# Two attention layers between two linear-attention layers: side work in pieces of three, an output projection in two parts, and the score bound as a bias of the exponential

## The chip, the cores and the metric

The kernel runs on one core of one Trainium2 chip. The core has a matrix engine (PE), a vector engine (DVE), a scalar engine that evaluates functions such as the exponential (ACT), a general engine (POOL) and an engine that in this kernel only starts transfers (SP). Each of them works through its own list of instructions in order; they wait for each other through semaphores. The metric is the device time of one launch in microseconds (us), lower is better.

## The reference

The input x has 2048 rows of 512 numbers. Four layers are applied one after the other, each to the row-normalized x, and each adds its result to x: attention A, linear attention B, attention A again, B again, with the same weights in both rounds.

```
x = x + A(layernorm(x));  x = x + B(layernorm(x))      (twice)

A:  q, k, v = split(x @ wqkv)                  32 heads of 16
    o = softmax(q k^T / 4) v;   result o @ wo
B:  q, k, v = split(x @ wqkv)
    phi(u) = [softmax(u w_phi), softmax(-u w_phi)]   per head
    kv = phi(k)^T v;  z = sum of phi(k)
    o = phi(q) kv / (phi(q) z + 1e-6);   result o @ wo
```

## The kernel before

**The attention.** The 32 heads are worked in four octets of eight, each octet in two groups of four heads (g = 0 to 7). For a group, the 2048 queries are taken in four blocks j of 512, and the 2048 keys in 16 tiles kt of 128. One (g, j, kt) is a step; a layer has 512 of them. The loop in `attention` (L862) issues for each step `scores` (L807), which is four matmuls of 64 rows into two PSUM tiles, each followed by one exponential on ACT over 128 x 1024 numbers (L816), and then `pvs` (L819) of the step two before (LAG), four matmuls of probabilities with values into one PSUM accumulator. After 16 steps the accumulator is divided by its row of sums on DVE (`norm`, L474); a finished octet's block goes to the DRAM buffer oD. The three PSUM tiles of scores are the only buffer between PE and ACT, so PE can be at most three exponentials ahead.

**The bound of the scores.** The kernel does not look for the maximum. It subtracts half of the squared norm of the query and half of the largest squared norm of a key. The queries, keys and these bounds sit in tiles kq of 64 rows for each head: 48 rows of high and low parts, one row `sh` with the bound (written by DMA, `load_shift`, L802) and 15 rows that are constant (DMA from dC, L781). So the subtraction is done by the score matmul itself, and the exponential has a constant scale and a constant bias of zero. The squared norms come from `square`, `norms`, `key_bound` and `add_bound` (L642 to L667). The lowest bound of every octet goes to `okt`; a flag at the end starts a second, general version of the kernel if a bound is too low.

**Side work.** Between the steps, PE also does what the next octets need, in pieces. `octet(o)` (L678) computes values (pieces of 16 matmuls of 128 x 128) and queries and keys (pieces of 4 x 4 matmuls, each 32 columns wide, L553); `prep_ao` and `prep_b` (first attention only) load, fold, scale and split the weights of the later layers; `tail(j)` (L846) does the output projection of block j over all four octets, adds x and computes the next layer's normalized and transposed input. These generators stand in a queue, `fill`; `pump` (L853) runs the first one up to its next `yield`. A credit grows by `rate` per step (0.38, 0.345 or 0.55) and a whole credit pays for one piece; after the 16th step of a block a piece is run in any case. At step 118 of an octet the rest of the next octet is run without pause and its kq tiles are loaded. All side work shares one PSUM bank, M. The weight preparation works on whole weights, for instance one DVE instruction over 128 x 2048 numbers (L91, L117, L120), right behind the loads that it reads.

**Order.** PE's order in the attention is the order of the program. The order on the other engines and on SP comes from a scheduler at build time; SP issues its transfers strictly in that order. Large tiles come from a pool of 11 buffers (`bigp`), and the tile stg, from which kq is loaded, has one buffer.

**The B layers.** After the last step, `feed` of layer B runs 16 tiles of 128 rows; between its first tiles it runs what is left of tail(3), three pieces of 4 x 4 matmuls for each tile. The end of B feeds the first octet of the next attention (`head`, `head_norms`, `feed_end`).

Of the kernel before, what the change touches and what calls it, by code (L numbers as in the profile page):

```python
# [17 lines left out]
P = 128  # L18
S = 2048
D = 512  # L20
# [10 lines left out]
SHROW = 16.0  # L31
# [4 lines left out]
FILLED = 118  # L36
# [7 lines left out]
def mha_hedgehog_stack(ctx, tc, x_in, a_wqkv, a_wo, b_wqkv, b_wphi, b_wo, out, shmin=SHMIN):  # L44
# [66 lines left out]
    def scale_of(vs, name):  # L111
        return scale_from([peak_of(v, None) for v in vs], name)

# [23 lines left out]
    xd = [tc.dram_tile([S, D], F32, name=f"xd{i}") for i in range(3)]  # L137
    oD = tc.dram_tile([NJ, P, 3, 2, 512], F16, name="oD")

    def split_store(w, sc, dram, name):  # L140
        hl = big([P, 2, NC4, 512], F16, name)
        split((hl[:, 0], hl[:, 1]), w, sc)
        nc.sync.dma_start(dram, hl)
        return hl


    dC = tc.dram_tile([16, 2, S], F16, name="dC")
    c16 = np_.tile([16, 2, 512], F16, tag="yt", name="c16", bufs=3)
    nc.gpsimd.memset(c16[:, 0, :], SHROW)
    nc.gpsimd.memset(c16[:, 1, :], 0.0)  # L150
# [10 lines left out]
    def prep_a():  # L161
# [7 lines left out]
        for j in range(NJ):  # L169
            nc.sync.dma_start(dC[:, :, j * 512:(j + 1) * 512], c16)  # L170
# [31 lines left out]
        with tc.manual_schedule(engines=COMPUTE):  # L202
# [42 lines left out]
            for j in range(1, NJ):  # L245
# [20 lines left out]
                a1.head_norms(j - 1)  # L266
# [9 lines left out]

    def prep_ao():
        wo = load_w(a_wo, "awo")
        es, sc = scale_of([flat(wo)], "sAo")
        split_store(wo, sc, dAo, "ahlo")  # L280
        con["oA"] = out_scale(con["esA"], es, "c_oA")
# [7 lines left out]

    perm_in = lambda ap: ap.rearrange("p (c h q f) -> p c q h f", c=4, h=4, q=2)  # L290
    perm_out = lambda ap: ap.rearrange("p (c q h f) -> p c q h f", c=4, h=4, q=2)

    def prep_b():
# [5 lines left out]
        yield  # L299
        folded = []  # L300
        for i in range(2):
            w = load_w(b_wqkv[:, i * 512:(i + 1) * 512], f"bw{i}")
            wf = big([P, NC4, 512], F32, f"bf{i}")
            for c in range(4):
# [10 lines left out]
                for q in range(2):  # L315
                    nc.vector.tensor_copy(
                        wf[:, :, c * P + q * 64:c * P + q * 64 + 64].rearrange("p n (h f) -> p n h f", f=DH),
                        psf.rearrange("p (n h q f) -> p n h q f", n=NC4, h=4, q=2)[:, :, :, q, :])
                yield
            folded.append(wf)  # L320
        es, sc = scale_of([flat(folded[0]), flat(folded[1])], "sB")
# [3 lines left out]
        for i in range(2):  # L325
            split_store(folded[i], sc, dBqk[:, i], f"bhl{i}")
            yield
        wv = load_w(b_wqkv[:, 1024:1536], "bwv")
        esv, scv = scale_of([flat(wv)], "sBv")
        hl = big([P, 2, NC4, 512], F16, "bhlv")  # L330
        for d in range(NC4):
            src, dh, dl = (perm_in(wv[:, d, :]), perm_out(hl[:, 0, d, :]), perm_out(hl[:, 1, d, :]))
            for c in range(4):
                for q in range(2):
                    split((dh[:, c, q], dl[:, c, q]), src[:, c, q], scv)
            yield
        for a in range(2):
            nc.sync.dma_start(dBv[a], hl[:, a])
        yield
        wo = load_w(b_wo, "bwo")  # L340
        eso, sco = scale_of([flat(wo)], "sBo")
        split_store(wo, sco, dBo, "bhlo")
# [170 lines left out]
    def o_block(j, ob, wo, co, x_src, x_dst, box, after=None, wide=True, early=False, piece=4):  # L513


        for t2 in range(2):
            r = (4 * j + 2 * t2) * P
            xt = xp.tile([P, 2, D], F32, tag="xt", name="xt")
            nc.sync.dma_start(xt, x_src[r:r + 2 * P, :].rearrange("(t p) d -> p t d", p=P))
            if wide:  # L520
                ps2 = psS.tile([P, 2, 512], F32, tag="S", name="po2")
            if early and t2 == 0:
                for cs in ((0,), (1,), (2,), (3,)):
                    for u in range(2):
                        for c in cs:
                            for i, (a, b) in enumerate(PASSES):
                                nc.tensor.matmul(ps2[:, u, :], ob[:, c, a, u * P:(u + 1) * P], wo[:, b, c, :],
                                                 start=(c == 0 and i == 0), stop=(c == NC4 - 1 and i == 2))
            for u in range(0 if early and t2 == 0 else 2):
                t = 2 * t2 + u  # L530
                n = 0
                for a, b in PASSES:
                    for c in range(NC4):
                        if n % piece == 0:
# [3 lines left out]
                        mm_cols(ps, ob[:, c, a, t * P:(t + 1) * P], wo[:, b, c, :], n, not wide)  # L538
# [10 lines left out]
    def mm_cols(ps, w, x, n, cols):  # L549

        for i in range(4 if cols else 1):
            r = slice(32 * i, 32 * i + 32) if cols else slice(0, P)
            nc.tensor.matmul(ps[r, :], w[:, r], x, start=(n == 0), stop=(n == 11), skip_group_check=cols)  # L553
# [29 lines left out]
    class LayerA:  # L583
# [23 lines left out]
        def stage(self, o):  # L607
            self.oct[o].update(
                stg=stgp.tile([P, 4, S], F16, tag="stg", name="stg"),
                sh=np_.tile([32, S], F16, tag="sh", name="sh", bufs=1),  # L610
                km=sp.tile([32, 4], F32, name="km"),
            )

        def project(self, o, j, ps, ten, piece=2):
            n = 0
            for a, b in PASSES:
                for c in range(NC4):
                    mm_cols(ps, self.oct[o]["w"][:, a, ten, c, :], self.xnT[j][:, b, c, :], n, piece == 4)
# [4 lines left out]
        def values(self, o, j, ps):  # L623
# [3 lines left out]
            for t in range(4):  # L627
                for a, b in PASSES:
                    for c in range(NC4):
# [3 lines left out]
                        if n % 16 == 0 and n < 48:  # L633
                            yield
# [7 lines left out]
        def square(self, hi):  # L642
            sq = np_.tile([P, 512], BF16, tag="sq", name="sq", bufs=3)
# [6 lines left out]
        def norms(self, o, j, sq, ten):  # L650
            q = self.oct[o]
            psn = psum1("psn")
            nc.tensor.matmul(psn[0:32, :], bones, sq, start=True, stop=True)
            if ten:
                nc.vector.tensor_reduce(q["km"][:, j:j + 1], psn[0:32, :], AX.X, ALU.max)
            else:
                nc.vector.tensor_scalar(q["sh"][:, j * 512:(j + 1) * 512], psn[0:32, :], -0.5 / SHROW, None, op0=ALU.mult)

        def key_bound(self, o):
            q = self.oct[o]  # L660
            q["hk"] = sp.tile([32, 1], F32, name="hk")
            nc.vector.tensor_reduce(q["hk"], q["km"], AX.X, ALU.max)
            nc.vector.tensor_scalar(q["hk"], q["hk"], -0.5 / SHROW, None, op0=ALU.mult)

        def add_bound(self, o, sl):
            q = self.oct[o]
            nc.vector.tensor_scalar(q["sh"][:, sl], q["sh"][:, sl], q["hk"], None, op0=ALU.add)  # L667

        def end_octet(self, o):
            self.key_bound(o)  # L670
            self.add_bound(o, slice(0, S))
            self.lowest(o)

        def lowest(self, o):
            i = self.li * 4 + o
            nc.vector.tensor_reduce(okt[:, i:i + 1], self.oct[o]["sh"], AX.X, ALU.min)

        def octet(self, o):  # L678
# [4 lines left out]
            for j in range(NJ):  # L683
                yield from self.values(o, j, psum1("pv_"))
                yield
            self.stage(o)
            stg = self.oct[o]["stg"]
            for j in range(NJ):
                for ten in (1, 0):
                    ps = psum1("pqk")  # L690
                    yield from self.project(o, j, ps, ten, 4)
# [6 lines left out]
                    sq = self.square(hi)  # L698
                    yield
                    self.norms(o, j, sq, ten)  # L700
                    if j == 2 and ten == 0:
                        self.alloc_pairs(2 * o)
                        self.load_rows(2 * o, slice(0, 1536))
                    if j < 3 or ten:
                        yield
            self.end_octet(o)
            self.ready = o
# [22 lines left out]
        def head_norms(self, j, tens=(1, 0)):  # L730
            for ten in tens:
                self.norms(0, j, self.sqs.pop((j, ten)), ten)
# [4 lines left out]
        def feed(self, lns, work):  # L737

            for j, (a, b, c) in enumerate(work):
# [4 lines left out]
                if j == NJ - 1:  # L744
                    self.head_norms(2)
# [3 lines left out]
                if 0 < j < NJ - 1:  # L749
                    self.head_norms(j - 1)  # L750
# [9 lines left out]
        def feed_end(self, more=True):  # L760
            self.head_norms(3, (1,))
            if more:
                self.head_values(2)
            self.key_bound(0)
            self.add_bound(0, slice(0, 512))
            self.load_shift(0, slice(0, 512))
            self.head_norms(3, (0,))
            self.head_values(3)
            self.add_bound(0, slice(512, S))
            self.load_rows(0, slice(1536, S))  # L770
            self.load_shift(0, slice(512, S))
            self.lowest(0)
            self.alloc_pairs(1)
            self.load_pairs(1)

        def alloc_pairs(self, g):
            tiles = []
            for pr in range(2):
                t = big([P, 2, S], F16, f"kq{g}_{pr}")
                for s in range(2):  # L780
                    nc.sync.dma_start(t[64 * s + 48:64 * s + 64], dC)  # L781
                tiles.append(t)
            self.kq[g] = tiles

        def load_pairs(self, g):
            self.load_rows(g, slice(0, S))
            self.load_shift(g, slice(0, S))
# [14 lines left out]
        def load_shift(self, g, sl):  # L802
            sh = self.oct[g // 2]["sh"]
# [484 lines left out]
```

## Time and profile before

| | us |
|---|---|
| median of 3 runs (2619.69 to 2622.96) | 2621.23 |
| the profiled execution's own time | 2620.91 |
| its span, first to last instruction | 2619.1 |
| PE busy | 2503.1 |
| ACT busy | 2196.1 |
| DVE busy | 997.4 |
| POOL busy | 371.5 |

Busy times are sums over the span; matmuls are pipelined, so PE's busy time holds overlaps and is no measure of how full it is. Times in rows of the timeline count from the start of the span. In a group's row stand the count, the busy time, the mean duration of one in ns, and the idle time before it with what ended it. A duration is longer than the distance between two starts, since consecutive instructions of an engine overlap a little.

### The profile page before, as it was taken

The page shows a single profiled execution, that of the slowest core. Times are in us where ns is not written, and L with a number is a line of the kernel's source. Part 1 is how long each engine was busy: PE and PEld are TensorE (multiplying, and loading weights), DVE is VectorE, ACT ScalarE, POOL GpSimd, SP SyncE. Part 2 cuts the span into 40 slices and gives each one's busy share as a digit, 9 for nine tenths or more (in the row PEclk, how much of TensorE's full clock was granted, in tenths as well). Part 3 has the DMA queues.
Part 4 walks back from the last instruction along what each step waited for, and adds up shares of the span by engine and source line. Part 5 has one row for each costly group of instructions (what it writes and reads, how often), then busy time and mean ns, then how long its engine had stood idle before and what let it go on. Part 6 is the DMA issues. An engine that isn't in the chain of part 4 may idle for free.

```text
span 2619.1 us, 50234 instructions
## 1 busy us (share of the span) xinstructions
PE 2503.1 (96%) x20960; PEld 812.9 (31%) x20960; DVE 997.4 (38%) x1902; ACT 2196.1 (84%) x2436; POOL 371.5 (14%) x502
## 2 busy tenths in 40 slices
PE   6899999999999899999899999999999999999998
PEld 4322222222223122355343222222222212224543
DVE  6211211221223533689872122112211302338897
ACT  5799999999899899654437999999999999994552
POOL 3000000000000000266430000000000000004552
PEclk8999999999999899999999999999999999999999
DMA  4500220130113411100234003201301230110003
GB/s 147 110 29 9 47 40 5 27 50 11 57 27 84 157 45 46 41 25 1 73 96 67 13 11 51 32 5 28 60 5 26 56 74 32 48 44 26 9 17 106
DMA packets 52414, 120.43 MB, mean 46 GB/s; under 512 B 11024, under 2 KB 14224, under 8 KB 49360
## 3 DMA queue, kind: packets, MB, share of 16 engines
q1 hardware_dynamic: 51504, 114.76, 18.3%
q8 instruction: 166, 2.72, 0.4%
q0 software_dynamic: 672, 2.36, 0.2%
q14 instruction: 72, 0.59, 0.1%
HBM read 60.06 MB, written 31.59 MB: 35 GB/s over the span
## 4 chain that ended last, share of the span: by engine, by line
PE 73%; DVE 12%; ACT 8%; issue 4%; POOL 2%; DMA 1%; ACTq 0%; SPq 0%; POOLq 0%; DVEq 0%
PE pv L831 33%; PE s L813 20%; ACT p L816 6%; PE pqk L553 5%; PE po L553 5%; DVE su L1017 2%; PE pk L946 1%; PE pbv L946 1%; PE pq L946 1%; POOL f L1026 1%; PE pst L419 1%; DVE f L1009 1%; PE pn L1086 1%; DVE su L1018 1%; DVE yt L503 1%
## 5 line engine op out<-in xcount | busy, mean ns | idle before, releaser
L816 ACT ACTIVATE p<-s 128x1024 f32<-128x1024 f32 x2048 | 1907.0, 1075 | 63.9 <-PE s L813 58.0
L831 PE MATMUL pv<-p,v 128*32 128x512 f32 x8192 | 1096.3, 607 | 13.8 <-DVE yt L476 13.7
L813 PE MATMUL s<-kq 64*128 64x512 f16 x4096 | 676.8, 384 | 23.2 <-DMA kq<-sh 2.8
L813 PEld LDWEIGHTS <-kq 64*128 64x128 f16 x4096 | 157.7, 93 | 805.6 <-issue 792.0
L831 PEld LDWEIGHTS pv<-p,v 128*32 128x32 f32 x8192 | 162.4, 108 | 370.9 <-issue 331.6
L645 POOL TENSOR_TENSOR sq<-stg 128x512 bf16<-128x512 f16 x48 | 68.9, 1435 | 1313.0 <-DVE stg L696 1306.1
L695 DVE TENSOR_SCALAR tq<-pqk,c_qk 128x512 f32<-128x512 f32 x48 | 35.1, 732 | 451.3 <-PE pqk L553 451.3
L1026 POOL TENSOR_TENSOR f<-f,su 128x1024 f32<-128x1024 f32 x62 | 120.0, 1935 | 575.7 <-DVE su L1020 547.4
L476 DVE STREAM_TRANSPOSE yt<-pv 128x512 f32<-128x512 f32 x64 | 45.8, 716 | 404.9 <-PE pv L831 404.8
L946 PEld LDWEIGHTS <-xnTa 128*128 128x128 f16 x1152 | 109.6, 98 | 139.8 <-DVE f L1010 14.8
L553 PEld LDWEIGHTS <-wA 128*32 128x32 f16 (+1 forms) x2496 | 86.4, 97 | 149.4 <-issue 100.6
L1011 ACT ACTIVATE f<-f,c_pB 128x1024 f32<-128x1024 f32 x64 | 72.5, 1148 | 38.2 <-DVE f L1010 37.9
L553 PE MATMUL pqk<-xnTb,wA 128*32 128x512 f16 (+1 forms) x1248 | 98.4, 381 | 1.1 <-ACT xnTb L429 1.1
L946 PE MATMUL pbv<-wbv,xnTa 128*128 128x512 f16 x384 | 88.2, 379 | 11.0 <-DVE f L1010 11.0
L553 PE MATMUL po<-woA,ob 128*32 128x512 f16 x1536 | 97.5, 379 | 0.0
L553 PE MATMUL pqk<-xnT,wA 128*32 128x512 f16 (+1 forms) x1224 | 92.4, 379 | 2.7 <-DVE xnT L432 2.2
L1032 ACT ACTIVATE fk<-f 128x1024 f16<-128x1024 f32 x30 | 31.7, 1057 | 74.9 <-POOL f L1026 74.9
L541 DVE SCALAR_TENSOR_TENSOR xt<-po,c_oA,xt 128x512 f32<-128x512 f32 x32 | 23.2, 724 | 183.9 <-PE po L553 183.9
L946 PE MATMUL pq<-wbqk,xnTa 128*128 128x512 f16 x384 | 88.4, 379 | 0.0
L946 PE MATMUL pk<-wbqk,xnTa 128*128 128x512 f16 x384 | 88.4, 379 | 0.0
L1058 ACT ACTIVATE qT<-pqt 128x512 f32<-128x512 f32 x64 | 34.7, 593 | 56.6 <-PE pqt L1057 56.6
L1017 DVE TENSOR_REDUCE su<-f 128x64 f32<-128x1024 f32 x64 | 77.5, 1210 | 9.7 <-ACT f L1011 8.9
(261 smaller groups left out, 1936.8 us busy)
## 6 DMA issues: line engine op xcount, KB each, us to landing
kq<-stg SPq DMA_DIRECT2D x96, 128.0 KB, 5.6
xd<-xt SPq DMA_DIRECT2D x24, 512.0 KB, 2.8
xt<-xd SPq DMA_DIRECT2D x24, 512.0 KB, 3.6
kq<-stg SPq DMA_DIRECT2D x96, 96.0 KB, 4.2
kq<-dC SPq DMA_DIRECT2D x64, 128.0 KB, 3.7
oD<-osp SPq DMA_DIRECT2D x24, 256.0 KB, 2.0
ob<-oD SPq DMA_DIRECT2D x8, 768.0 KB, 5.4
xt<-in_A_x_dram SPq DMA_DIRECT2D x8, 512.0 KB, 3.9
```

What stands on the lines that cost most here:

```text
L476: nc.vector.transpose(yt.rearrange("p a b -> p (a b)"), ps)
L553: nc.tensor.matmul(ps[r, :], w[:, r], x, start=(n == 0), stop=(n == 11), skip_group_check=cols)
L645: nc.gpsimd.tensor_tensor(sq, hi, hi, ALU.mult)
L695: nc.vector.tensor_scalar(tq, ps, cqk, CLAMP, op0=ALU.mult, op1=ALU.min)
L813: nc.tensor.matmul(s[:, u, :], t[r:r + 64, 0, kt * P:(kt + 1) * P], t[r:r + 64, 1, j * 512:(j + 1) * 512], start=True, stop=True)
L816: nc.scalar.activation(pt, s, AF.Exp, scale=0.25 / (QS * QS))
L831: nc.tensor.matmul(acc[32 * hh:32 * hh + 32, :], self.oct[o]["v"][:, r:r + 32], pt[:, hh % 2, :], start=(kt == 0), stop=(kt == NT - 1), sk ...
L946: nc.tensor.matmul(dst, xnT[:, a, c, t * P:(t + 1) * P], w(b, c), start=(i == 0 and c == 0), stop=(i == 2 and c == NC4 - 1))
L1011: nc.scalar.activation(f, f, AF.Exp, scale=con["pB"])
L1017: nc.vector.tensor_reduce(su, f[:, r, :], AX.X, ALU.add)
L1026: nc.gpsimd.tensor_tensor(f3, f3, self.part_sums(f3, slice(0, 64), factor), ALU.mult)
L1058: nc.scalar.activation(qT[i][:, :, t * P:(t + 1) * P], pst.rearrange("p (g t) -> p g t", g=4), AF.Copy)
```

## The change

1. **Bound as bias.** The rows `sh` and dC are gone; kq has 48 used rows (ROWS), and the score matmuls read 48 rows instead of 64. Squared norms of queries and keys of two blocks go into one PSUM tile (four matmuls, 32 columns each), one DVE reduction takes their maximum, and after the second pair `bound` takes the maximum over all partitions on POOL and makes one number per octet, the same in all 128 partitions of a tile `bias` of 128 x 1. The exponential gets `bias=` that tile.
2. **Thirds.** Pieces are of 3 x 4 matmuls of 32 columns (before 4 x 4) and of 12 value matmuls (before 16). The rate is 0.5, then 0.45 in the second attention, and 0.48, 0.6, 0.66 in the first. A generator can yield a step number before which it is not continued, or FREE for a piece without PE work, which is run without credit. Octet o's queries and keys do not start before step 4 of octet o - 1. Its kq tiles are loaded whole at step 116.
3. **Output projection in two parts.** As soon as octets 0 to 2 of block j are done, `part(j)` is queued: it loads them from oD, multiplies them with their three quarters of wo, adds x and writes the sum to the layer's result in DRAM. `tail(j)` reads that back and adds the fourth octet alone, 3 x 4 matmuls for each 128 rows. DRAM rows are split into tiles of 256 rows (class Rows). tail(3) between the first tiles of B now has one piece of 3 x 4 matmuls for each tile.
4. **Weights in parts.** Peaks and splits of the weights are done by quarters with FREE yields, five FREE yields stand between a load and its first use, the folding writes with one DVE copy instead of two, and the permutation of heads is put into the load of wo of B, which becomes eight transfers of 16 partitions, instead of into 64 small DVE instructions.

```
-                nc.scalar.activation(pt, s, AF.Exp, scale=0.25 / (QS * QS))
+                nc.scalar.activation(pt, s, AF.Exp, scale=0.25 / (QS * QS), bias=self.oct[g // 2]["bias"])
...
+        def bound(self, o):
+            q = self.oct[o]
+            m = sp.tile([P, 1], F32, name="nmx")
+            nc.vector.tensor_tensor(m, q["nm"][:, 0:1], q["nm"][:, 1:2], ALU.max)
+            mm = sp.tile([P, 1], F32, name="nma")
+            nc.gpsimd.partition_all_reduce(mm, m, P, bass_isa.ReduceOp.max)
+            q["bias"] = sp.tile([P, 1], F32, name="bias")
+            nc.vector.tensor_scalar(q["bias"], mm, -0.25 / (QS * QS), None, op0=ALU.mult)
...
+        def part(self, j):
+            if j == 0:
+                self.wo = load_hl(dAo, "woA")
+            ob = big([P, 3, 2, 512], F16, f"ob{j}")
+            nc.sync.dma_start(ob, oD[j])
+            yield
+            yield from o_block(j, [ob[:, c] for c in range(3)], self.wo, con["oA"], self.x_src, self.x_dst, [],
+                               wide=False, cs=range(3))
...
-            yield from o_block(j, ob, self.wo, con["oA"], self.x_src, self.x_dst, xts, ln.half, wide=False)
+            yield from o_block(j, {3: ob}, self.wo, con["oA"], self.x_dst, self.x_dst, xts, ln.half, wide=False, cs=(3,))
...
+    def split_parts(w, sc, name, *drams):
+        hl = big([P, 2, NC4, 512], F16, name)
+        for d in range(NC4):
+            split((hl[:, 0, d], hl[:, 1, d]), w[:, d], sc)
+            yield FREE
...
+        wo = big([P, NC4, 512], F32, "bwo")
+        for h in range(4):
+            for q in range(2):
+                r = h * 32 + q * DH
+                nc.sync.dma_start(wo[r:r + DH], b_wo.rearrange("(c q h d) n -> q h d c n", q=2, h=4, d=DH)[q, h])
+        yield from landing()
...
-                    rate = 0.55 if self.ready == 3 else 0.38 if n < FILLED else 0.345
-                    credit = min(credit + rate, 2)
-                    if credit >= 1 or turn:
-                        credit -= 1
-                        self.pump(1)
+                    credit = min(credit + rate(n), 3)
+                    if credit >= 1 or turn or self.fill and self.fill[0][1] == FREE:
+                        credit -= self.pump(n)
```

More of the change, by code (lines that the diff above doesn't have):

```diff
@@ L136, in mha_hedgehog_stack, with __init__, __getitem__ @@
     dBo = tc.dram_tile([P, 2, NC4, 512], F16, name="dBo")
-    xd = [tc.dram_tile([S, D], F32, name=f"xd{i}") for i in range(3)]
-    oD = tc.dram_tile([NJ, P, 3, 2, 512], F16, name="oD")
[L140 to L150, printed above, removed]
+    class Rows:
+        def __init__(self, name):
+            self.tiles = [tc.dram_tile([2 * P, D], F32, name=f"{name}_{i}") for i in range(NT // 2)]
+        def __getitem__(self, key):
+            return self.tiles[key[0].start // (2 * P)]
+    xd = [Rows(f"xd{i}") for i in range(3)]
+    oD = tc.dram_tile([NJ, P, 3, 2, 512], F16, name="oD")
     con = {}
@@ L325, in prep_b @@
         for i in range(2):
-            split_store(folded[i], sc, dBqk[:, i], f"bhl{i}")
-            yield
+            yield from split_parts(folded[i], sc, f"bhl{i}", dBqk[:, i])
         wv = load_w(b_wqkv[:, 1024:1536], "bwv")
[L329 to L342, printed above, removed]
+        yield from landing()
+        esv, scv = scale_from((yield from peaks([wv])), "sBv")
+        yield from split_parts(wv, scv, "bhlv", *[dBv[a] for a in range(2)])
+        wo = big([P, NC4, 512], F32, "bwo")
[3 more added lines that the diff above has]
+                nc.sync.dma_start(wo[r:r + DH], b_wo.rearrange("(c q h d) n -> q h d c n", q=2, h=4, d=DH)[q, h])
+        yield from landing()
+        eso, sco = scale_from((yield from peaks([wo])), "sBo")
+        yield from split_parts(wo, sco, "bhlo", dBo)
         con["oB"] = out_scale(esv, eso, "c_oB")
@@ L510, in norm2, with o_block, load @@
         finish_o(yn, dst)
-    def o_block(j, ob, wo, co, x_src, x_dst, box, after=None, wide=True, early=False, piece=4):
-        for t2 in range(2):
+    def o_block(j, ob, wo, co, x_src, x_dst, box, after=None, wide=True, early=False, cs=range(NC4)):
+        def load(t2):
             r = (4 * j + 2 * t2) * P
@@ L519, in o_block @@
             nc.sync.dma_start(xt, x_src[r:r + 2 * P, :].rearrange("(t p) d -> p t d", p=P))
+            return xt
+        xt2 = [] if wide else [load(0), load(1)]
+        for t2 in range(2):
+            r = (4 * j + 2 * t2) * P
+            xt = load(t2) if wide else xt2[t2]
             if wide:
@@ L531, in o_block @@
                 n = 0
-                for a, b in PASSES:
-                    for c in range(NC4):
-                        if n % piece == 0:
+                for c in cs:
+                    for a, b in PASSES:
+                        if n % (4 if wide else 3) == 0:
                             yield
@@ L760, in feed_end @@
         def feed_end(self, more=True):
-            self.head_norms(3, (1,))
+            self.load_rows(0, slice(1536, S))
             if more:
                 self.head_values(2)
[L764 to L772, printed above, removed]
+            last = self.values(0, 3, psum1("pv_"))
+            for _ in range(1 if more else 3):
+                next(last)
+            self.head_norms(1)
+            self.bound(0)
+            run(last)
             self.alloc_pairs(1)
-            self.load_pairs(1)
+            self.load_rows(1, slice(0, S))
         def alloc_pairs(self, g):
[L777 to L787, printed above, removed]
+            self.kq[g] = [big([P, 2, S], F16, f"kq{g}_{pr}") for pr in range(2)]
         def pair_rows(self, g):
@@ L853, in pump, with more, pumps @@
         def pump(self, n):
+            while self.fill and self.fill[0][1] <= n:
+                free = self.fill[0][1] == FREE
+                try:
+                    self.fill[0][1] = next(self.fill[0][0]) or 0
+                    if self.fill[0][1] <= n:
+                        return not free
+                except StopIteration:
+                    self.fill.popleft()
+            return False
+        def more(self, gen):
+            self.fill.append([gen, 0])
+        def pumps(self, n):
             for _ in range(n):
@@ L1219, in attention @@
                 ln = Norm(xts, f"{self.name}_{j}")
[L1220 removed]
+                run(o_block(j, [ob[:, c] for c in range(NC4)], wo, con["oA"], self.x_src, self.x_dst, xts, ln.half))
                 nxt.feed(j, ln.all())
```

203 lines of the change are left out of this document (96 added, 107 removed).

## The prediction

> **What bounds the kernel now.** I read the stages first, by busy times in windows cut at the first and last exponential of each attention.
>
> ```profile
> 84.40:1079.70 995.30, 969.81 (x8601) 259.02 (x8600) 250.57 (x551) 954.34 (x1024) 36.67 (x34) 0.99 0.21 48
> 1079.70:1391.00 311.30, 286.70 (x1938) 149.16 (x1931) 265.52 (x440) 135.27 (x181) 148.74 (x240) 0.98 0.16 45
> 1391.00:2363.70 972.70, 957.08 (x8511) 251.31 (x8509) 204.46 (x436) 952.61 (x1025) 36.23 (x31) 1.00 0.18 36
> 2363.70:2619.10 255.40, 237.37 (x1564) 119.32 (x1556) 219.52 (x345) 108.67 (x142) 123.57 (x124) 0.99 0.12 40
> ```
>
> The columns are length, then PE, weight loads, DVE, ACT and POOL busy. The two attentions are 1968 of the 2619 us, and in both PE and ACT are over 95% busy. Then the page's chain of waits, and its group of exponentials:
>
> ```profile
> PE 73%; DVE 12%; ACT 8%; issue 4%; POOL 2%; DMA 1%; ACTq 0%; SPq 0%; POOLq 0%; DVEq 0%
> ...
> L816 ACT ACTIVATE p<-s 128x1024 f32<-128x1024 f32 x2048 | 1907.0, 1075 | 63.9 <-PE s L813 58.0
> ```
>
> The chain names PE for 73%, yet busy shares cannot separate two engines that are both nearly full. So I looked for what each takes when it does not wait. ACT first, in the timeline of a stretch without side work:
>
> ```profile
> 2087.47 51.43 ACT L816 ACTIVATE p<-s 128x1024 f32<-128x1024 f32 x56
> ...
> 2137.20 4.46 ACT L816 ACTIVATE p<-s 128x1024 f32<-128x1024 f32 x4
> ```
>
> The first of the 56 starts at 2087.47, the last at 2137.20: 49.73 / 55 = 0.904 us from start to start. So 1024 exponentials need 925.7 us, and that is the floor of an attention; the first stands 69.6 us above it, the second 47.0. Then PE:
>
> ```profile
> 1684.15 0.60 PE L813 MATMUL s<-kq 64*128 64x512 f16 x4
> ...
> 1685.68 0.60 PE L813 MATMUL s<-kq 64*128 64x512 f16 x4
> ...
> 1688.75 1.05 PE L553 MATMUL pqk<-xnTb,wA 128*32 128x512 f16 x16
> 1689.73 0.60 PE L813 MATMUL s<-kq 64*128 64x512 f16 x4
> ```
>
> A step without a piece is 1.53 us of PE (1685.68 - 1684.15) against 1.808 of ACT (two exponentials). A piece of 4 x 4 matmuls holds PE about 0.98 - 0.12 = 0.86 us, of which 0.12 is the change back to scores that a step has anyway. Step plus piece is 2.39: longer than ACT's step, and PE can be only three exponentials ahead. So the excess is PE's pieces coming in lumps, plus waits of the weight preparation, the longest of which is here:
>
> ```profile
> 895.57 1.94 ACT L816 ACTIVATE p<-s 128x1024 f32<-128x1024 f32 x2 [10.40 <-PE s L813]
> ```
>
> The floor is ACT's. What raises the price of one exponential counts 2048 times; what smooths PE can win back at most 69.6 + 47.0 = 116.6 us.
>
> **The change part by part.** *The bias.* The exponential had a constant scale and a constant bias; now its bias is read from a tile of 128 x 1, one number per partition. No exponential of the trace has that, but other ACT instructions have such operands.
>
> ```profile
> 10.12 1.51 ACT L406 ACTIVATE xn<-xb,lb,ly 128x512 f32<-128x512 f32 x2
> 11.53 1.04 ACT L89 ACTIVATE pkj<-awk 128x1024 f32<-128x1024 f32 x1
> ...
> 64.34 1.91 ACT L429 ACTIVATE xnT<-pst 128x1024 f16<-128x1024 f32 x2
> 66.15 0.62 ACT L647 ACTIVATE sq<-stg 128x512 bf16<-128x512 f16 x1
> 66.67 0.58 ACT L640 ACTIVATE v<-pv__781 128x512 f32<-128x512 f32 x1
> 67.14 0.71 ACT L182 ACTIVATE wsc<-awk,sA_sc 128x512 f32<-128x512 f32 x1
> 67.76 0.71 ACT L183 ACTIVATE wA_s<-awk,sA_sc 128x512 f16<-128x512 f32 x1
> ...
> L1011 ACT ACTIVATE f<-f,c_pB 128x1024 f32<-128x1024 f32 x64 | 72.5, 1148 | 38.2 <-DVE f L1010 37.9
> ...
> L1032 ACT ACTIVATE fk<-f 128x1024 f16<-128x1024 f32 x30 | 31.7, 1057 | 74.9 <-POOL f L1026 74.9
> ```
>
> Over 512 numbers from SBUF, start to start without waiting: no such operand 0.52 us (L647, 66.15 to 66.67), one (a scale, L182) 0.62, two (scale and bias, L406) 1.41 / 2 = 0.705. Each operand adds about 0.093, and they are not hidden although the engine runs without a gap. Over 1024 the exponential with a scale operand takes 1148 ns against 1057 for a copy without: 91. The exponential reads PSUM, as L429 does (1.81 / 2 = 0.905, the same as L816), and no row has PSUM with an operand. Bounds: nothing, if the read hides behind the instruction before; 0.079, the smallest difference that I find (709 ns of L183 against 630 of L495, copies of one shape):
>
> ```profile
> L183 ACT ACTIVATE wA_s<-awk,sA_sc 128x512 f16<-128x512 f32 x3 | 2.1, 709 | 0.0
> ...
> L495 ACT ACTIVATE obB<-yb 128x512 f16<-128x512 f32 x32 | 20.1, 630 | 40.6 <-DVE yb L491 40.6
> ```
>
> and 0.094 at the top. I take 0.093, since the two steps between back-to-back rows agree on it and one of them adds a bias: 0.997 a piece, 1024 x 0.997 = 1020.9 us for an attention.
>
> The Trainium skill, "ScalarE: Activation LUTs", section "What ACT_TABLE_LOAD costs", speaks against this part: each [128,1] pointer operand adds about 93 ns to an ACTIVATE, and consecutive ones overlap by about 93 ns. The differences above agree with the first. By its full formula one exponential with a pointer bias would come every 1.04 us, and the sum would be some 88 us higher than mine; the trace's 0.904 for the constant form is already below its 0.946, so the measurement decides.
>
> *Thirds and rate.* At 1.994 us a step, PE needs 1.53, plus at most 0.66 pieces of 0.65 (three quarters of 0.86), 1.96 together. PE now has room, the stalls from lumps go, and what is late next is ACT itself. The whole gain of this part, as large as the excess above, is swallowed: it pays only below a floor that has moved up by 95 us for each attention.
>
> *48 rows.* Nothing: a score matmul of 64 rows lasts as long as one of 128 rows and the same 512 columns, so rows don't set it.
>
> ```profile
> L813 PE MATMUL s<-kq 64*128 64x512 f16 x4096 | 676.8, 384 | 23.2 <-DMA kq<-sh 2.8
> ...
> L946 PE MATMUL pk<-wbqk,xnTa 128*128 128x512 f16 x384 | 88.4, 379 | 0.0
> ```
>
> *Norms and bound.* Twelve DVE operations per octet become five, and one POOL reduction is added; for octets 1 to 3 they end at least 20 steps before their use, for octet 0 beside the last value matmuls. DVE is a quarter busy in the attentions (first window row). I count 0; the cover gone, some 2 us in each layer. The 64 loads from dC that go kept no engine waiting in these rows but at the start (below).
>
> *The parts' loads: two new waits.* `part(0)` is queued when block 0 of octet 2 is done, and its first matmul needs oD[0] back from DRAM. In the second attention nothing else stands in the queue, and the changed program's order has this matmul two steps behind the accumulation's end.
>
> ```profile
> 2029.69 0.72 DVE L476 STREAM_TRANSPOSE yt<-pv 128x512 f32<-128x512 f32 x1 [2.82 <-PE pv L831]
> ...
> 2033.32 0.34 SPq L841 DMA_DIRECT2D oD<-osp  x1
> ```
>
> From the normalization to the store's issue 3.6 us, the store 2.0 and the load 5.4 (rows below): 11.0, with handovers 11.6. PE arrives after two steps, 4.0. Behind the waiting matmul stand the next scores, so ACT runs dry: 8 us.
>
> In the first attention `part(0)` comes behind the weights. In the changed order SP issues the load of ob0 behind the store of the last weight, and DVE splits the value weight of B only behind the normalization of the last block of octet 2. From there: normalization 3.6, split 1.28 + 2.35, eight issues for wo at 0.6, their landing, peak to store of wo, landing of ob0.
>
> ```profile
> 85.34 0.59 SPq L798 DMA_DIRECT2D kq<-stg  x1
> ...
> 892.87 2.24 DVE L91 TENSOR_REDUCE pk<-bwo 128x1 f32<-128x2048 f32 x1
> ...
> 897.95 1.28 DVE L117 TENSOR_SCALAR bhlo<-bwo,sBo_sc 128x2048 f16<-128x2048 f32 x1
> ...
> 899.27 2.35 DVE L120 SCALAR_TENSOR_TENSOR bhlo<-bwo,sBo_sc,bhlo 128x2048 f16<-128x2048 f32 x1
> ...
> 901.64 0.32 SPq L143 DMA_DIRECT2D dBo<-bhlo  x1
> ```
>
> ```profile
> kq<-stg SPq DMA_DIRECT2D x96, 128.0 KB, 5.6
> ...
> oD<-osp SPq DMA_DIRECT2D x24, 256.0 KB, 2.0
> ob<-oD SPq DMA_DIRECT2D x8, 768.0 KB, 5.4
> ...
> bwo<-in_B_wo_dram SPq DMA_DIRECT2D x1, 1024.0 KB, 10.1
> ```
>
> The parts of wo are 128 KB on 16 partitions, like kq: 5.6 (at most 10.1, the whole). Peak to store was 8.8 with 1 us of another normalization in it: 7.8. Sum 3.6 + 3.6 + 4.8 + 5.6 + 7.8 + 5.4 + 1.2 for handovers = 32. PE reaches that matmul six steps behind the last accumulation, 12 us: a wait of 20 (5 more with the longer landing). The weights in parts take the old 10.4 us stall away, but this stands in its place.
>
> At the end of the first attention the rate of 0.66 leaves 0.03 us a step; a wait for DVE before a transpose shows. I allow 5 us (0 to 10).
>
> *B layers.* tail(3) has 3 x 4 matmuls between the tiles instead of 12 x 4:
>
> ```profile
> 1089.64 2.70 PE po L553 x48
> ```
>
> that is 2.0 us less for each of four tiles, 8; DVE is 85% busy there, so I count 3 for each B layer (0 to 8).
>
> *Starts of the attentions.* The first started behind the load of `sh`; the other rows of kq landed just then too:
>
> ```profile
> 83.65 2.50 PE L813 MATMUL s<-kq 64*128 64x512 f16 x8 [2.76 <-DMA kq<-sh]
> 83.72 0.48 PEld L813 LDWEIGHTS <-kq 64*128 64x128 f16 x3 [2.81 <-DMA kq<-stg]
> ```
>
> so 1 us gained, and 2 us in the second for shorter norms.
>
> *Sum.* First attention 1020.9 + 20 + 5 + 1 (its first steps) = 1047 against 995.3: +52. Second 1020.9 + 8 + 1 = 1030 against 972.7: +57. B layers -6, starts -3. The profiled execution took 2620.9, 0.3 below the median shown: 2620.9 + 100 = **2721**, I say 2720.
>
> **The rivals.** *The operand is hidden* behind the preceding exponential (the other side: faster). For it: no row has an exponential from PSUM with an operand. Against: L182, L183 and L406 run without gaps and still pay. Then the floor stays 925.7, and PE decides: 512 x 1.53 plus some 200 pieces at 0.65 is about 920, so the second attention takes the floor, the wait of 8 and a third of today's 47 us excess, 950; the first the same with 20 for 8, the 5, and 16 weight pieces of 0.5 us, 975 to 985. Together 33 to 43 less, B and starts 9 less: about 2575. The point at which it turns: with an operand above 0.02 us the gain is gone. *The operand costs 0.079*: 2048 x 0.014 = 29 less, 2692. *The two waits don't show*, because transfers land sooner or the scheduler's order matters less than I read: 28 less, 2692. *The first wait is longer*, its transfers queued behind the 2 MB load of B's weights that the same order puts there: 5 to 20 more, 2725 to 2740. That the change does not do what it says is in the forecast: PE's steadier rate moves nothing once ACT is the bound.
>
> **How the numbers follow.** Forecast 0.50; operand at 0.079 0.16; waits absent 0.11; first wait longer 0.15; hidden 0.07; the rest 0.01. The range runs from 2680, both cheaper cases, to 2745; hidden is left out, and so is a mixture of the cheaper two (2664); as each case spreads by some 10 us, about 8 in 10 are inside. A measurement of this kernel tells about 0.2% from no change; only the hidden case is faster, and nothing but a partly hidden operand is within: faster 0.07, same 0.01, slower 0.92.
>
> **What would show it.** The exponentials' start to start in a quiet stretch: 0.997, or 0.904 if I am wrong on the main term. Windows of about 1047 and 1030 us with ACT busy nearly throughout. Two waits of PE's first po matmul for DMA, 20 and 8 us, and few others. The first four tiles of B up to 2 us closer together. A faster kernel would mean that the operand is free; 2690 that one of the two terms is smaller.

## The result and the profile after

| | before | after |
|---|---|---|
| median of 4 runs, us | 2621.31 (2619.69 to 2622.96) | 2747.09 (2742.62 to 2749.26) |
| ratio, 95% interval | | 1.0478 (1.0459 to 1.0496) |
| profiled execution, its span | 2620.91, 2619.1 | 2742.62, 2740.8 |

The changed kernel is 4.8% slower. The forecast was 2720 with a range to 2745: the direction and the main term were right, the sum was 27 us too low, and the measured time lies 2 us above the range. The windows of the changed kernel, cut like those of before (length, then PE, weight loads, DVE, ACT and POOL busy):

```profile
78.57:1144.29 1065.72, 995.34 (x8754) 271.56 (x8754) 245.27 (x540) 1031.79 (x1024) 37.70 (x38) 0.98 0.21 49
1144.29:1449.31 305.02, 276.06 (x1780) 144.33 (x1779) 257.90 (x430) 133.80 (x178) 148.79 (x243) 0.98 0.16 45
1449.31:2486.30 1036.99, 984.56 (x8658) 262.76 (x8653) 200.57 (x431) 1029.04 (x1025) 35.62 (x32) 1.00 0.17 38
2486.30:2740.80 254.50, 231.47 (x1414) 115.63 (x1412) 219.10 (x345) 108.63 (x141) 123.43 (x124) 0.98 0.12 40
```

The attentions grew by 70.4 and 64.3 us, and ACT, at 954 and 953 us before, is now busy for 1032 and 1029. On the page, the chain that ended last and the group of exponentials:

```profile
PE 44%; ACT 36%; DVE 12%; issue 5%; POOL 2%; DMA 1%; SPq 1%; ACTq 0%; POOLq 0%; DVEq 0%
...
L804 ACT ACTIVATE p<-s,bias 128x1024 f32<-128x1024 f32 x2048 | 2060.8, 1394 | 45.5 <-PE s L801 40.9
```

ACT's share of the chain rose from 8% to 36%, nearly all of it from PE. The mean duration in the group (1394 ns, before 1075) overstates the price, since an exponential overlaps the one before it. The price shows in starts. ACT's timeline in a stretch where PE has no side work:

```profile
847.77 26.65 ACT L804 ACTIVATE p<-s,bias 128x1024 f32<-128x1024 f32 x26
...
860.72 13.70 ACT L804 ACTIVATE p<-s,bias 128x1024 f32<-128x1024 f32 x13
```

The second row is the same run of exponentials from a later point on: 13 of the 26 are left, so 13 lie between 847.77 and 860.72, 0.996 us each (before 0.904, forecast 0.997). PE's longest single waits in the first attention, then the longest in the second (us in all, how many, longest):

```profile
PE po L572 <- DMA ob<-oD: 22.7, 1, 22.7
PE s L801 <- DMA kq<-stg: 5.2, 2, 4.0
...
PE po L572 <- DMA ob<-oD: 6.0, 1, 6.0
```

Both forecast waits are there, each once. How they arrive at the exponentials, by ACT's timeline: 23.27 and 6.59 us without work.

```profile
897.68 2.12 ACT L804 ACTIVATE p<-s,bias 128x1024 f32<-128x1024 f32 x2 [23.27 <-PE s L801]
...
2139.22 2.12 ACT L804 ACTIVATE p<-s,bias 128x1024 f32<-128x1024 f32 x2 [6.59 <-PE s L801]
```

### The profile page after: what moved, and what is told of

It is laid out like the page before. It is cut to its first block, busy times and chain, and to the rows that moved or that the text cites. A ratio compares the mean times of both kernels' runs of the same rounds, so it can differ in the third digit from the quotient of the medians.

```text
span 2740.8 us, 49983 instructions
## 1 busy us (share of the span) xinstructions
PE 2537.9 (93%) x20960; PEld 826.3 (30%) x20960; DVE 974.1 (36%) x1868; ACT 2348.6 (86%) x2434; POOL 371.2 (14%) x508
## 4 chain that ended last, share of the span: by engine, by line
PE 44%; ACT 36%; DVE 12%; issue 5%; POOL 2%; DMA 1%; SPq 1%; ACTq 0%; POOLq 0%; DVEq 0%
ACT p L804 34%; PE pv L816 15%; PE s L801 14%; PE po L572 4%; PE pqk L572 2%; DVE su L1031 2%; PE pbv L960 1%; PE pk L960 1%; PE pq L960 1%; DVE f L1023 1%; DVE f L1024 1%; POOL f L1040 1%; DVE mx L1020 1%; DVE su L1032 1%; DVE st L376 1%
## 5 line engine op out<-in xcount | busy, mean ns | idle before, releaser
L804 ACT ACTIVATE p<-s,bias 128x1024 f32<-128x1024 f32 x2048 | 2060.8, 1394 | 45.5 <-PE s L801 40.9
L801 PE MATMUL s<-kq 48*128 48x512 f16 x4096 | 718.5, 383 | 92.1 <-ACT p L804 58.0
L801 PEld LDWEIGHTS <-kq 48*128 48x128 f16 x4096 | 175.5, 93 | 876.8 <-issue 858.8
L560 DVE SCALAR_TENSOR_TENSOR xt<-po,c_oA,xt 128x512 f32<-128x512 f32 x64 | 47.2, 738 | 292.7 <-PE po L572 292.7
L572 PE MATMUL po<-woA,ob 128*32 128x512 f16 x1152 | 81.2, 385 | 28.8 <-DMA ob<-oD 28.8
## 6 DMA issues: line engine op xcount, KB each, us to landing
wbqk<-dBqk SPq DMA_DIRECT2D x2, 2048.0 KB, 12.6
```

The lines of the kernel that those rows point to most:

```text
L801: nc.tensor.matmul(s[:, u, :], t[r:r + ROWS, 0, kt * P:(kt + 1) * P], t[r:r + ROWS, 1, j * 512:(j + 1) * 512], start=True, stop=True)
L804: nc.scalar.activation(pt, s, AF.Exp, scale=0.25 / (QS * QS), bias=self.oct[g // 2]["bias"])
```

## The experiments

Theory: reading a 128 x 1 operand raises ACT's floor, and two waits for ob0 add to it; the rest of the change gains a little. Rivals: the operand is free and the rest of the change is slow; the waits cannot be moved by order.

### The operand alone

The kernel before with a tile of zeros as bias (e1_before_operand), and the changed kernel with a constant bias (e2_after_no_operand).

```
-  nc.scalar.activation(pt, s, AF.Exp, scale=0.25 / (QS * QS))
+  nc.scalar.activation(pt, s, AF.Exp, scale=0.25 / (QS * QS), bias=zb)        # e1, zb: zeros
...
-  nc.scalar.activation(pt, s, AF.Exp, scale=..., bias=self.oct[g // 2]["bias"])
+  nc.scalar.activation(pt, s, AF.Exp, scale=...)                              # e2
```

> The kernel before, with one thing added: the exponential reads its bias from a 128 x 1 tile that holds zeros. Theory (the operand sets the time): exponentials in a quiet stretch 0.996 us from start to start, as in the changed kernel (0.904 before). The attentions then stand at 1020 us of exponentials plus the waits that the kernel before has anyway (10 for the weights, 3 at the start, some 15 for the pieces run without pause): 1040 and 1028 against 995 and 973, together about 2720. Rival (the 48 rows, the thirds or the parts make the changed kernel slow, and the operand only happens to be there): about 2621, no change. The steadier pieces are worth something below the raised floor: then this kernel is slower than that, 2740 or more.

Measured: 2739.12 us, ratio to the kernel before 1.0457 (1.0439 to 1.0474). Its attentions:

```profile
85.20:1136.59 1051.39, 987.41 (x8602) 271.82 (x8600) 250.69 (x551) 1031.85 (x1024) 36.61 (x34) 0.99 0.19 45
...
1447.08:2481.90 1034.82, 973.78 (x8514) 262.89 (x8509) 204.43 (x436) 1030.16 (x1025) 36.22 (x31) 1.00 0.16 34
```

One operand of zeros makes the kernel before 119 us slower, nearly as slow as the whole change. The median distance of exponentials is 0.996, as expected; the windows are 11 and 7 longer than I expected. Against back-to-back exponentials, steps 16 to 330 of its first attention lose 14.2 us (5.5 in the changed kernel), so PE's lumps still cost something under the higher floor.

> The changed kernel with a constant bias of zero: the bound is still worked out, but it isn't subtracted before the exponential, so all exponentials of a query are larger by the same factor, which the division takes out again. Theory: exponentials at 0.904 in quiet stretches, ACT's floor 926 again, and PE's steps and pieces decide: attentions of about 985 and 950 with the two waits for ob0 (24 and 9 us) still there, in all 2575 to 2600. Rival (the operand costs nothing, the parts and thirds do): 2740, no change from the changed kernel.

Measured: 2616.46 us, 0.9988 (0.9978 to 0.9997). The operand is thus worth 130.6 us in the changed kernel. But 2575 to 2600 was too good. The attentions took 1013 and 964 us, and PE's timeline in a stretch of the second shows why (rows without waits, a piece in every second step):

```profile
1561.35 0.61 PE L801 MATMUL s<-kq 48*128 48x512 f16 x4
...
1565.07 0.60 PE L801 MATMUL s<-kq 48*128 48x512 f16 x4
...
1568.78 0.61 PE L801 MATMUL s<-kq 48*128 48x512 f16 x4
```

These are two steps apart: 3.72 us for PE, against 4 x 0.904 = 3.616 for ACT. Where pieces run at a rate near 0.5, PE is the bound once the operand is gone.

### Which operand, and how many

e8_scale_operand reads the scale from a tile instead of the bias; e7_two_operands reads both from tiles. The times are of one run each.

```
+  sct = cp.tile([P, 1], F32, name="sct")
+  nc.vector.memset(sct, 0.25 / (QS * QS))
...
+  nc.scalar.activation(pt, s, AF.Exp, scale=sct)                                    # e8
+  nc.scalar.activation(pt, s, AF.Exp, scale=sct, bias=self.oct[g // 2]["bias"])     # e7
```

> The changed kernel with the scale read from a 128 x 1 tile instead of the bias, which is a constant zero (the bound isn't subtracted; the division takes that out). Theory (the price is that of an operand, whichever it is): 0.996 us from start to start and 2743. Rival (only the bias costs): 0.904 and 2613, as without an operand.

> The changed kernel with the scale of the exponential read from a 128 x 1 tile as well, of the same value. Theory (each operand adds its 0.092 us, one by one): 1.088 us from start to start, 2047 x 0.092 = 188 more, about 2930. Rival (the first operand switches the engine to another way of reading, the second costs nothing more): 2743.

Measured: 2747.24 and 2921.17 us. The second attentions, e8 then e7:

```profile
1452.13:2489.76 1037.63, 985.26 (x8657) 262.71 (x8653) 200.54 (x431) 1029.07 (x1025) 35.63 (x32) 1.00 0.17 38
```

```profile
1534.35:2664.80 1130.45, 989.10 (x8659) 276.68 (x8654) 200.41 (x431) 1122.85 (x1025) 35.64 (x32) 1.00 0.16 35
```

A scale costs what a bias costs, and a second operand adds (1130.45 - 1037.63) / 1024 = 0.091 us again. The operands are priced one by one, the scale as much as the bias, and a tile of zeros (e1_before_operand) as much as the bound.

### The waits: more steps between load and use

e3_after_no_wait with the operand, e4_after_neither without it.

```
             nc.sync.dma_start(ob, oD[j])
+            for _ in range(14 if self.first and j == 0 else 5):
+                yield FREE
             yield
...
-  rate = lambda n: 0.48 if n < 2 * STEPS else 0.6 if n < 400 else 0.66
+  rate = lambda n: 0.48 if n < 2 * STEPS else 0.6 if n < 400 else 0.75
```

> The changed kernel with its operand; the first matmul of part(0) comes 14 steps after the issue of its load in the first attention instead of at once, that of every other part 5 steps after it, and the rate at the end of the first attention is 0.75 instead of 0.66 so that the side work still ends inside it. Theory: the PE waits of 22.7 and 6.0 us for ob0 go, the exponential gaps of 25 and 10 with them, and the time is 2747 - 24 - 9 = 2714, or up to 8 more if the rate of 0.75 makes PE late at the end of the first attention. Rival (the wait only moves, because the transfers of ob0 stand behind the others in the queue whatever PE does): 2735 to 2747.

> Both edits together: the changed kernel without the operand (the bound isn't subtracted, the division takes that out) and without the two waits. Theory (the two terms are independent): that of the kernel without the operand less about 30, so 2545 to 2570, below the kernel before. Rival (with the floor down, PE has no room for the same rate of pieces, so that the waits' gain is lost again at the end of the first attention): within 10 us of the kernel without the operand alone.

Measured: 2733.09 (1.0435; 1.0417 to 1.0452) and 2602.73 (0.9937; 0.9920 to 0.9954), each 14 us less than without the edit, not 30: in neither run does the theory's range hold, nor the rival's. The second attention lost its wait (1029.5 us). In the first, PE came 14 steps later and still waited 9.1 us. DVE, SP and PE in that stretch of e3_after_no_wait:

```profile
892.58 0.72 DVE L490 STREAM_TRANSPOSE yt<-pv 128x512 f32<-128x512 f32 x1 [24.30 <-PE pv L816]
...
894.20 2.46 DVE L277 TENSOR_REDUCE pk<-bwo 128x1 f32<-128x512 f32 x4
```

```profile
902.70 0.32 SPq L295 DMA_DIRECT2D dBo<-bhlo  x1
903.11 2.42 SPq L838 DMA_DIRECT2D ob<-oD  x3
```

```profile
909.67 1.47 PE L572 MATMUL po<-woA,ob 128*32 128x512 f16 x12 [9.12 <-DMA ob<-oD]
```

In the changed kernel the same peaks began at 880.15; here they begin at 894.20. DVE stood idle for 24 us, because in its list they now come behind the normalization of the next block, for which PE finished the sums at 892.5. SP's load of ob0 waits behind the store that needs these peaks. More distance on PE moved the load as well. The end of the first attention, with its rate of 0.75, got longer as well: the last 72 steps take 10.6 us more than back-to-back exponentials (5.3 in the changed kernel), and without the operand 21.5 (14.3 in e2_after_no_operand).

### The waits: order of the queue

e5_after_queue (with the operand) and e6_after_queue_no_operand put wo of B behind part(0).

```
+        if j == 0 and self.first:
+            self.more(prep_bo())        # peaks and split of wo of B, taken out of prep_b
```

> The changed kernel with its operand; the preparation of wo of B stands behind part(0) in the queue instead of ahead of it, so that SP issues the loads of woA and ob0 ahead of the loads and the store of that weight; eight steps lie between part(0)'s load and its first matmul, five for the other parts, and the rate at the end of the first attention is 0.75. Theory (the first wait comes from the order on SP and DVE: ob0's load behind dBo's store, and that behind the peaks of bwo): no PE wait for ob0 above 2 us, both gaps of 25 and 9 us gone, and 2 to 5 us lost at the end of the first attention by the higher rate, as with the waits shortened: 2716 to 2720. Rival (the wait is the transfers' own time, or only the number of steps counts): a wait of 5 us or more at the first po matmul, 2725 to 2733 as there.

> The same order of the queue with a constant bias of zero (the bound isn't subtracted; the division takes that out). Theory: 2616 without the operand, less the gaps of 28 and 9.7 us, and 5 lost at the end: 2583, 1.4% below the kernel before. Rival (PE is the bound there, and the time that it waited is made up by the pieces it then has to run later): 2595 to 2603, as with the waits shortened.

Measured: 2731.27 (1.0426; 1.0409 to 1.0444) and 2607.86 (0.9956; 0.9939 to 0.9973). Both theories miss; the first number is the rival's, the second lies above the rival's too. PE waited 12.6 us for ob0, and 12.8 without the operand. DVE, then SP, of e5_after_queue:

```profile
860.16 0.72 DVE L495 STREAM_TRANSPOSE yt<-pv 128x512 f32<-128x512 f32 x1 [28.55 <-PE pv L821]
...
863.69 0.87 DVE L116 TENSOR_SCALAR bhlv<-bwv,sBv_sc 128x512 f16<-128x512 f32 x2
```

```profile
866.71 1.65 SPq L298 DMA_DIRECT2D dBv<-bhlv  x2
868.41 0.45 SPq L581 DMA_DIRECT2D woA<-dAo  x1
868.95 0.74 SPq L845 DMA_DIRECT2D ob<-oD  x1
```

The same pattern, one weight earlier: the split of the value weight stands in DVE's list behind a normalization (28.55 us idle), the stores of its result on SP behind that, and ob0's load behind the stores. PE reached its matmul at 864.1, 4.8 us before that load was issued, and the load took 7.7. Whether order or the landing itself makes the wait, this run can't tell; the next can.

### The waits: off the chain

In e9_after_side and e10_after_side_no_operand both weights leave the queue.

```
+            side = prep_bvo() if extra is not None else iter(())   # value weight and wo of B
...
+                    if n >= 392:
+                        next(side, None)
...
+            for _ in range(10 if j == 0 else 5):
+                yield FREE
```

> The changed kernel with its operand; in the first attention the preparation of the value weight and of wo of B no longer stands ahead of part(0): it has no PE work, and runs one piece a step beside the other side work from step 392 on. So the loads of woA and ob0 are issued behind the stores of dBqk, ahead of everything that waits for the normalization at step 385; ten steps lie between part(0)'s load and its first matmul, five for the other parts. Theory (what PE waited for, in the changed kernel and with both earlier edits, is ob0's load behind a store of SP whose data DVE makes only behind that normalization; it doesn't depend on the number of steps alone): no wait for ob0 above 2 us, the gaps of 25 and 9 gone, 2747 - 34 = 2713. Rival (ob0's landing is slow by itself, or PE's own order makes the gap): a gap of 10 or more again, 2725 or more.

> The same order with a constant bias of zero (the bound isn't subtracted; the division takes that out). Theory: 2608, as with the queue's order changed and no operand, less the 16 us of the gap at step 387 that is left there, and some 4 at the end of the first attention, where the rate is 0.66 again: 2586 to 2592, over 1% below the kernel before. Rival (PE is the bound there, and pieces that it would have run in the gap only come later): 2600 to 2608.

Measured: 2715.17 (1.0361; 1.0344 to 1.0379) and 2585.11 (0.9867; 0.9851 to 0.9884), both within 2 us of what was expected. SP of e9_after_side, ahead of the kq loads of the next octet:

```profile
807.81 4.56 SPq L295 DMA_DIRECT2D dBqk<-bhl  x2
812.47 0.37 SPq L839 DMA_DIRECT2D ob<-oD  x1
```

and, besides short ones for ACT (at most 0.4 us), PE's longest waits in its first attention, none of them for ob any more:

```profile
PE s L802 <- DMA kq<-stg: 5.9, 2, 3.8
PE po L573 <- DVE xt L561: 4.5, 2, 4.3
```

Here ob0 took 7.1 us to land, no less than before, so the landing by itself is not the reason. The 4.3 us are new: the addition of x stands on DVE behind the split that was moved. The edit is worth 32 us, with the operand (2747.1 to 2715.2) and without (2616.5 to 2585.1). Not all of it is the two waits: in the profiled executions with the operand (27 us apart), the stretch of the first wait (steps 384 to 440) gives 17.8, the second attention 6.7 and the last 72 steps of the first 3.5.

### A bound that is a number

e11_after_side_constant is that order with `bias=-8.0` in place of the tile: a shift that is the same for all scores.

> The order with the side queue, and a bound that is a number in the program, the same for all octets: the exponential's bias is the constant -8 instead of the tile. (A common shift of all scores is taken out by the division.) Theory (the price is that of reading a 128 x 1 operand, not of a bias that is not zero): 0.904 us from start to start and 2585, as with a constant of zero. Rival (a bias other than zero is read from a tile anyway): 0.996 and 2715.

Measured: 2586.63 us, 0.9872 (0.9855 to 0.9888), exponentials at 0.904. The bias of -8 is free as a number in the program. This and e10_after_side_no_operand take 1.3% less than the kernel before; what they give up is the bound worked out from the data.

## Why the prediction was right in its main term and wrong in its sum

The terms of the profiled execution. The distances from start to start of all exponentials in the changed kernel's trace, each less 0.996, were added up by steps. A late start is a distance that is 0.01 to 0.045 us too long.

| term | predicted | measured |
|---|---|---|
| to the first exponential | -1 | -5.9 |
| first attention: 1024 exponentials | 1020.9 | 1019.9 |
| its first wait (steps 389 to 393) | 20 | 25.2 |
| its first steps | 1 | 5.1 |
| its end (from step 440) | 5 | 4.8 |
| late starts (206 of them) | 0 | 3.7 |
| folding of weights (330 to 355), smaller gaps, end of the last exponential | 0 | 7.0 |
| **first attention** | **1047** | **1065.7** |
| first B and start of the second attention | -5 | -6.3 |
| second attention: 1024 exponentials | 1020.9 | 1019.9 |
| its wait | 8 | 8.7 |
| late starts (260 of them, 4.6), smaller gaps, end of the last exponential | 1 | 8.4 |
| **second attention** | **1030** | **1037.0** |
| second B | -3 | -0.9 |

**The operand** was right to 1%: 0.092 us for each, not hidden. The Trainium skill, "ScalarE: Activation LUTs", section "What ACT_TABLE_LOAD costs", gives about 93 ns per [128,1] pointer operand; the runs agree for one operand and for two. An estimate by its whole formula makes the period 1.04; the trace has 0.996.

**The first wait** was forecast by its mechanism and mis-sized by 5 us: 25.2 for 20. The chain of waits between 860.85 and 895.57 was the one in the forecast, 34.7 us long instead of 32. Two of its pieces were longer: DVE's peaks began 6.9 us behind the last issue of bwo (5.6 taken), and ob0 took 6.5 (5.4). The 5.6 was the median of kq's transfers, but the eight of bwo, issued 0.5 us apart, landed 1.0 apart, so that the last took 7.2. The other 2.5 is what ACT loses behind the wait, since PE runs its piece of `po` before it returns to scores. The rival "first wait longer" has the amount, at its smallest, but not the reason: the 2 MB load had landed at 885.1, ahead of ob0's issue at 889.06, and bwo's parts landed 1.0 apart from the first two on, which were there before that load was issued.

```profile
873.22 6.94 DMA oD<-osp
880.16 2.46 DVE pk L277 x4
...
889.06 6.46 DMA ob<-oD
895.53 0.04 issue
895.57 1.47 PE po L572 x6
```

The first row names the store issued last; the peaks behind it read bwo, issued just ahead.

**"PE now has room, the stalls from lumps go"** is the step that failed, by some 18 us over both attentions; I counted 1 us for all of it. The forecast set an average, 1.96 us of PE a step, against ACT's 1.994. But a step that has a piece takes PE 1.53 + 0.65 = 2.18, and pieces come in steps that follow each other. PE's scores in the changed kernel, at steps 261 to 263, with a piece between each two:

```profile
607.13 0.60 PE L801 MATMUL s<-kq 48*128 48x512 f16 x4
...
609.31 0.61 PE L801 MATMUL s<-kq 48*128 48x512 f16 x4
...
611.49 0.60 PE L801 MATMUL s<-kq 48*128 48x512 f16 x4
```

2.18 us from step to step, and ACT follows with pairs of distances of 1.17 and 1.01. After a few such steps the three buffers are empty. Each of the small gaps (over 0.045 us; 3.5 us in the first attention, 3.0 in the second) has such a piece just before the scores that ACT waited for, and so have the gaps of the folding (3.4).

The late starts are two things. In 194 of the 466 the second of the two exponentials began only 0.10 us behind the end of its scores: it waited for PE, about 4 us in all. In the other 272 the first of the two did, and the next came 0.016 us later than from a full queue, 4 us in all. The trace before has these too (189 and 185 late starts of 0.017, 345 of them behind such a first exponential), so this part of the excess could be seen there. That such a start causes the 0.016 was read from the traces and not tested.

**Starts and B.** The first exponential came 5.9 us earlier, but PE then waited 5.2 for kq, so the first 16 steps gave it back: together -0.8, forecast 0. In the first B layer the first two distances between tiles were 2.4 and 0.9 us shorter (8.6 and 11.3 between starts, before 11.0 and 12.2), but the fifth gave it back (13.9 for 10.4). The last tile starts 160.4 us behind the end of the last exponential, before 161.0: B won 0.6, and the other 5.7 of the 6.3 come from the start of the second attention.

**The rest.** These terms are 21.6 us over the forecast. Of the 27, another 4.5 is that the profiled execution (2742.62) was the shortest of its four, and 0.9 that I rounded 2720.9 down.

**The rival "hidden operand"** is refuted: the operand is paid in full. What it expected of the rest of the change can be read from e2_after_no_operand, and it was too good: 2575 forecast, 2616 measured. I compared PE's sum over an attention (920; the numbers given add up to 913) with ACT's (926), the same mistake as above. Side work is not spread evenly; where pieces are dense PE needs 3.72 for ACT's 3.616, and what PE saves elsewhere cannot be stored beyond three exponentials.

**The value of the thirds** is small, as forecast: an undisturbed octet of the first attention takes 256.9 us here and 258.9 with lumps and operand (e1_before_operand). That difference holds all of the change but the operand; the thirds alone were not run.

## What to carry to other kernels

Where one engine runs an instruction thousands of times, price each operand of it first: a bias read from a tile cost 119 to 131 us here, and one given as a number (0 or -8) nothing that shows. A wait for a transfer is found by walking the queues back from it, through SP's order and the list of the engine that makes the data; two edits that only moved PE's arrival or one neighbour left 9.1 and 12.6 of its 22.7 us, and the one that took the load out of the chain removed it. Compare two engines step by step where the buffer between them is short: sums and averages over a stage hide which is late.

## What the runs showed of the hardware

A [128,1] operand of an exponential that reads 128 x 1024 numbers from PSUM costs 0.092 us, scale or bias, and a second one 0.094 more (0.904, 0.996, 1.090 from start to start). Behind an exponential that began only 0.10 us after its scores, the next came 0.016 us late (272 of 2046 distances in the changed kernel). Eight loads of 128 KB on 16 partitions each, issued 0.5 us apart, landed 1.0 apart (about 130 GB/s), and four of 768 KB on 128 partitions in the same stretch 1.9 apart (about 415).
